# Retention of a chunk in 64-token halves on 64x64 quarters of TensorE, with a state in mid-chunk

## The chip, the cores and the metric

One core of a Trainium2 chip runs the whole kernel as one program. The metric is the device time of that program in microseconds (us). The kernel before was timed three times; the median is 195.26 us.

## The reference, cut to what matters

Retention (linear attention with a decay per head) over 4 batches, 8 heads, 768 tokens, 64 wide, and then a feed-forward part with a Mish activation:

```
for t in range(S):
    state = gamma[h] * state + outer(k[:, :, t], v[:, :, t])      # one 64x64 state a head
    y[:, :, t] = scale * (q[:, :, t] @ state)
x = y.transpose(0, 2, 1, 3).reshape(3072, 512)
h = x @ w_in                      # 512 x 2048
g = h * tanh(softplus(h))         # mish
out = g @ w_out                   # 2048 x 512
```

## The kernel before, in words

The 768 tokens of a batch are cut into 6 chunks of 128 tokens, so there are 24 chunks; chunks 0, 6, 12 and 18 begin a batch. Block 0 takes four chunks, and ten further blocks take two chunks (256 tokens) each. The retention of the next block is woven into the feed-forward part of the current one. The schedule is manual: each engine executes its instructions in the order in which the program writes them, and tiles of a pool take the buffer that was released first.

Retention of a chunk `g` works with these parts. q and k are cast and scaled by powers of gamma (`cast_q`, `cast_v` on GpSimd; `bring_k` is a GpSimd DMA that casts k) and turned on the DMA (`turn_by_dma`). `scores` (L437) multiplies k by q for each head, 64 rows by 128 columns, with 128 tokens moving; `mask` (L447) multiplies the 128x128 scores of 8 heads by the triangle on VectorE, and this is one instruction of 1024 columns a chunk. `y_two` (L535) then makes y for two chunks in one PSUM tile: `present` (L507) multiplies v by the masked scores (128 rows by 64 columns), `outer_two` makes k^T v of two later chunks (`outer`, L454, also 128x64), and `past` (L488) adds the state of the chunk before times q (64x64). ScalarE copies the whole of y into the tile `xt` (L545). The state goes on by `state_sum` (VectorE, L470) and `state_decay` (GpSimd, L475).

The feed-forward part of a block uses a Strassen-like scheme with seven products in place of eight. `g1_seven` makes h: products named first to seventh, each with a half `.0` and a half `.1` of 8 matmuls with 128 columns moving. `snap` copies a product from PSUM (ScalarE, L699; the one of `fifth.0` on VectorE, L697), `plus` adds it to a later product on VectorE (L709, the steps c11, c22, c12), and `mish_of` applies Mish on ScalarE (L704, the steps g11, g22, g12). The string `ORDER` fixes the order. `seven` then makes the output with seven products of 8 matmuls with 256 columns moving (L830); it needs sums of g that VectorE makes (`sums_a`, L618 and L619; `sums_b`, L792; `sums_c`, L796). `x_sums` (L650) makes sums of x from `xt` for the next block.

Between the steps the dictionaries of `steps_of` and `steps_of_first` call other work at named places: `at1` to `at6` within `g1_seven`, and `g7`, `m1`, `m5`, `m6`, `m2`, `m7`, `m3` within `seven`. In the kernel before, `m1` holds the scores of the next block, `m7` holds `y_two` and `m3` holds `x_sums`. PSUM has a pool `mmps` of 4 tiles of one bank (tag mm) and a pool `atps` of 2 tiles of two banks (tag at).

Of the kernel before, what the change touches and what calls it, by code (L numbers as in the profile page):

```python
# [16 lines left out]
def kernel(  # L17
# [9 lines left out]
    nc = tc.nc  # L27
# [29 lines left out]

    cpool = ctx.enter_context(tc.tile_pool(name="rn_const", bufs=1))
# [37 lines left out]

    tri_first = cpool.tile([P, R, C], FP32, name="tri_first")
# [9 lines left out]
    for h in range(H):  # L107
        o = 64 * (h % 2)
        nc.vector.memset(gcm[o:o + 64, h // 2, o:o + 64], float(gamma[h] ** C))
        nc.vector.memset(gcf[o:o + 64, h // 2:h // 2 + 1], float(gamma[h] ** C))  # L110
        o = 64 * (h // HP)
        nc.vector.memset(gcv[o:o + 64, h % HP:h % HP + 1], float(gamma[h] ** C))
    decay = gcv.unsqueeze(2).broadcast_to((P, HP, D))
# [7 lines left out]
    stcs = {}  # L121
# [9 lines left out]
    last_ended = []  # L131
# [61 lines left out]
    def cast_wout(s, on_act=0):  # L193
# [5 lines left out]
        for f in range(n, FPS, 2):  # L199
            nc.scalar.copy(t[:, f:f + 2], src[:, f:f + 2])  # L200

# [74 lines left out]

    def toks(c):
        return slice(c * HB, (c + 1) * HB)
# [167 lines left out]

    def mask(g):  # L447
# [6 lines left out]
    def outer(g, u_ps):  # L454
        _, k16, v16, _ = cast[g]
        for j in range(HP):
            for x in range(2):
                nc.tensor.matmul(  # L458
                    u_ps[64 * x:64 * x + 64, j], k16[:, 2 * j + x], v16[:, HP * x + j],
                    start=j == 0, stop=True, skip_group_check=True)  # L460
        us[g] = u_ps

    def state_sum(g):
        u_ps = us.pop(g)
        if g % NCH == 0:
            stcs[g] = stp.tile([P, HP, D], FP16, name="stc", tag="stc")
            nc.vector.tensor_tensor(stcs[g], u_ps, decay, op=ALU.mult)
        else:
            sus[g] = stp.tile([P, HP, D], FP32, name="suc", tag="suc")
            nc.vector.tensor_tensor(sus[g], u_ps, stcs[g - 1], op=ALU.add)  # L470
# [54 lines left out]
    def handed_on(blk):  # L525
        return [g for g in (first[blk] + 1, first[blk] + 2) if g < NCK and not last_of_batch(g)]

    def outer_two(blk):
        gs = handed_on(blk)
        if gs:  # L530
            u_ps = u_tile()
        for j, g in enumerate(gs):
            outer(g, u_ps[:, j, :, :D])

    def y_two(blk):  # L535
# [4 lines left out]
        outer_two(blk)  # L540
        for j in range(2):
            if (a + j) % NCH > 0:
                past(a + j, lambda i: y_ps[:, i, j])
        xts[blk] = xtp.tile([P, HP, TB], FP16, name="xt")
        nc.scalar.copy(  # L545
            xts[blk][:, :, :2 * C], y_ps.rearrange("p i j c -> p i (j c)"))
# [18 lines left out]
    def xt(blk, bp):  # L565
        return xts[0][:, :, bp] if blk == 0 else xts[blk][:, bp, :BLOCKS[blk] * C]
# [79 lines left out]
    def x_part(blk, i, j):  # L646
        n = NBP // 2
        return xts[blk][:, i * n:(i + 1) * n, j * P:(j + 1) * P]

    def x_sums(blk):  # L650
# [7 lines left out]

    ORDER = """
        first.0 second.0 at1 c11.0 first.1 second.1 g11.0 at2 c11.1 sixth.0 g11.1 fifth.0 at3  # L660
        sixth.1 fifth.1 seventh.0 c22.0 third.0 c12.0 g22.0 g12.0 at4
        seventh.1 c22.1 third.1 c12.1 g22.1 g12.1 at5 fourth.0 at6"""
    def g1_seven(blk, steps):
        n = NBP // 2
        gt = gtiles[blk, 0] = gp.tile([P, NFB, 2 * P], FP16, name="g", tag="g")
        for fb in range(NFB):
            gts[blk, fb] = gt[:, fb]
        both = atps.tile([P, 2, FPS, P], FP32, name="h_ps", tag="at")
        pb, px, pe, px1 = [
            mmps.tile([P, FPS, P], FP32, name="h_ps", tag="mm") for _ in range(4)]  # L670
        pb, px, pe = [pb, both[:, 0]], [px, px1], [pe, both[:, 1]]
# [66 lines left out]
        def _(g):  # L738
            mm(pe, g, s(1), t(1), True)
            m5[g] = snap(pe[g], g == 0)  # L740
# [57 lines left out]
    def seven(blk, steps, last, rest):  # L798
# [3 lines left out]
        px = [mmps.tile([P, wide], FP32, name="o_ps", tag="mm") for _ in range(parts)]  # L802
        if last:
            pe = atps.tile([P, 2, d_model], FP32, name="o_ps", tag="at")
            pb, pe = pe[:, 0, :hf], pe[:, 1, :hf]
        else:
            pe = mmps.tile([P, hf], FP32, name="o_ps", tag="mm")
# [28 lines left out]
        def snap(o_ps):  # L836
            x = op.tile([P, hf], FP32, name="snap", tag="snap", bufs=3)
# [4 lines left out]
        def store_now(i, j, c):  # L842
            row0, c = (first[blk] + i) * P, slice(j * hf + c.start, j * hf + c.stop)
            nc.sync.dma_start(out[row0:row0 + P, c], osb[i][:, c])

        def done(i, j, o_ps, plus=None):
            dst = osb[i][:, j * hf:(j + 1) * hf]
            for t, c in pieces(o_ps):
                if plus is None:
                    nc.vector.tensor_copy(dst[:, c], t)  # L850
# [12 lines left out]
        step("m1")  # L863
        rest()
        if not last:
            pb = mmps.tile([P, hf], FP32, name="o_ps", tag="mm")
# [5 lines left out]
        step("m6")  # L872
        mm(pb, a(0, 1), b(1, 0), True)
        done(0, 0, pb, m1)
# [7 lines left out]
        if last:  # L882
            def end(t, c):
                nc.vector.tensor_copy(osb[1][:, c], t)
                store_now(1, 0, c)

            mm(px, a(1, 1), tm(4), then=end)
        else:
            mm(px, a(1, 1), tm(4))
            done(1, 0, px)  # L890
            for i in range(2):
                row0 = (first[blk] + i) * P
                stores.append((1 + i, out[row0:row0 + P], osb[i]))


# [151 lines left out]
    def first_g2():  # L1047
# [5 lines left out]
        m5 = [op.tile([P, hf], FP32, name="snap", tag="snap", bufs=3) for _ in pairs]  # L1053
# [97 lines left out]
        for p, i in ends:  # L1151
            if (p, i) == (0, 1):
                y_two(1)
            end(p, i, 1)
            if (p, i) != ends[-1]:
# [4 lines left out]
        last_ended.append(lambda: ended(*ends[-1]))  # L1160
# [5 lines left out]

    def sum_next(g):
# [95 lines left out]
```

## Time and profile before

| | |
|---|---|
| median of 3 runs | 195.26 us (194.86 to 377.15) |
| time of the profiled execution | 195.58 us |
| its span | 193.6 us |
| PE busy | 186.7 us (96%) |
| VectorE busy | 162.0 us (84%) |
| ScalarE busy | 119.5 us (62%) |
| GpSimd busy | 91.5 us (47%) |
| granted clock | 1.0 |

The span runs from the first to the last instruction in the trace; the time of the execution has some 2 us more around it. PE is TensorE's matmuls, PEld its weight loads, DVE is VectorE, ACT ScalarE, POOL GpSimd, SP the engine that issues most DMAs.

### The profile page before, as it was taken

The numbers are of one execution on the slowest core, as the hardware profiler recorded it, in microseconds if no ns is written. First come the engines' busy times: TensorE is split into PE (matmuls) and PEld (weight loads), VectorE is DVE, ScalarE is ACT, GpSimd is POOL, SyncE is SP. The second block draws the span as 40 slices with busy tenths as digits, with TensorE's granted clock in tenths as the row PEclk, the third lists the DMA queues.
The fourth block names the chain that finished last, engine by engine and source line by source line (L and its number), as shares of the span: only waits on it lengthen the run. The fifth ranks groups of instructions, "written<-read, shape, count | busy, mean of one in ns | idle before, by whom it ended". The sixth has DMA issues, their size and how long they took to land.

```text
span 193.6 us, 6554 instructions
## 1 busy us (share of the span) xinstructions
PE 186.7 (96%) x2722; PEld 157.6 (81%) x2722; DVE 162.0 (84%) x329; ACT 119.5 (62%) x217; POOL 91.5 (47%) x135
## 2 busy tenths in 40 slices
PE   6999999999999999999999999999999999999992
PEld 2467645885988988988988988988988988988982
DVE  3787799989798997897897997897897997897871
ACT  3464798463793692782782882882873863964950
POOL 4280206596657756916905907907807914110000
PEclk9999999999999999999999999999999999999999
DMA  5999999995899999995995996994995993201103
GB/s 166 351 372 405 404 408 249 308 247 57 118 204 240 132 314 227 177 183 142 187 183 135 203 158 150 185 193 129 175 188 145 191 138 77 94 0 61 51 3 108
DMA packets 95805, 36.10 MB, mean 187 GB/s; under 512 B 82592, under 2 KB 89376, under 8 KB 95776
## 3 DMA queue, kind: packets, MB, share of 16 engines
q1 hardware_dynamic: 74544, 33.04, 67.2%
q0 software_dynamic: 21088, 2.62, 22.3%
q8 instruction: 21, 0.34, 0.7%
q14 instruction: 8, 0.07, 0.1%
q10 hardware_dynamic: 144, 0.03, 0.1%
HBM read 27.30 MB, written 6.29 MB: 174 GB/s over the span
## 4 chain that ended last, share of the span: by engine, by line
PE 85%; DVE 8%; issue 2%; ACT 1%; POOL 0%; POOLq 0%; DVEq 0%
PE h_ps L689 32%; PE o_ps L830 32%; PE o_ps L1072 5%; PE y_ps L512 3%; PE at L443 3%; DVE wsum L643 3%; PE at L419 2%; PE o_ps L1131 2%; PE h_ps L922 2%; PE y_ps L503 1%; DVE am L295 1%; PE u_ps L458 1%; DVE win L190 1%; DVE hsum L709 1%; DVE wout L198 1%
## 5 line engine op out<-in xcount | busy, mean ns | idle before, releaser
L709 DVE TENSOR_TENSOR hsum<-h_ps,hsnap 128x512 f32<-128x512 f32 x60 | 38.5, 685 | 6.0 <-PE h_ps L689 3.7
L704 ACT ACTIVATE g<-hsum 128x512 f16<-128x512 f32 x60 | 36.9, 631 | 4.0 <-DVE hsum L709 4.0
L699 ACT COPY hsnap<-h_ps 128x512 f32<-128x512 f32 x50 | 28.1, 583 | 14.8 <-PE h_ps L689 14.8
L689 PEld LDWEIGHTS <-wsum 128*128 128x128 f16 x640 | 36.4, 98 | 0.4
L830 PEld LDWEIGHTS <-gsum 128*128 128x128 f16 x336 | 30.3, 98 | 4.4 <-DVE gsum L618 0.5
L689 PE MATMUL h_ps<-xsum,wsum 128*128 128x128 f16 x480 | 30.4, 219 | 0.0
L830 PE MATMUL o_ps<-tmat,gsum 128*128 128x256 f16 (+1 forms) x256 | 29.7, 266 | 0.2 <-DVE gsum L618 0.2
L689 PEld LDWEIGHTS <-win 128*128 128x128 f16 x480 | 28.1, 98 | 1.4
L388 POOL DMA_DIRECT2D qk<-in_k_dram x36 | 27.9, 776 | 0.0
L401 POOL COPY gate<-gsum 128x1 f16<-128x1 f16 x18 | 3.4, 186 | 50.8 <-DVE gsum L792 39.7
L545 ACT CAST xt<-y_ps 128x1024 f16<-128x1024 f32 x10 | 10.1, 1012 | 25.2 <-PE y_ps L503 22.2
L830 PEld LDWEIGHTS <-g 128*128 128x128 f16 x256 | 23.4, 98 | 2.3
L449 DVE TENSOR_TENSOR am<-at,tri 128x1024 f16<-128x1024 f32 x20 | 24.3, 1218 | 0.3 <-PE at L443 0.3
L393 POOL TENSOR_TENSOR v<-vf,qvs 128x512 f16<-128x512 f32 x20 | 21.3, 1067 | 2.0 <-DMA vf<-in_v_dram 1.9
L852 DVE TENSOR_TENSOR osb<-o_ps,snap 128x256 f32<-128x256 f32 (+1 forms) x31 | 12.0, 412 | 11.5 <-ACT xt L545 9.8
L376 POOL TENSOR_TENSOR qk<-qf,qvs 128x512 f16<-128x512 f32 x20 | 21.4, 1068 | 0.0
L830 PE MATMUL o_ps<-wout,g 128*128 128x256 f16 (+1 forms) x168 | 20.8, 267 | 0.0
L689 PE MATMUL h_ps<-xt,win 128*128 128x128 f16 x320 | 19.5, 219 | 0.0
L839 ACT COPY snap<-o_ps 128x256 f32<-128x256 f32 (+1 forms) x32 | 11.4, 358 | 6.3 <-PE o_ps L830 6.3
L689 PE MATMUL h_ps<-xsum,win 128*128 128x128 f16 x160 | 12.3, 220 | 0.0
L689 PE MATMUL h_ps<-xt,wsum 128*128 128x128 f16 x160 | 12.2, 219 | 0.0
L704 ACT ACTIVATE g<-h_ps 128x512 f16<-128x512 f32 x20 | 11.9, 595 | 0.0
(124 smaller groups left out, 282.8 us busy)
## 6 DMA issues: line engine op xcount, KB each, us to landing
vf<-in_v_dram SPq DMA_DIRECT2D x24, 256.0 KB, 5.0
out_dram<-osb SPq DMA_DIRECT2D x22, 256.0 KB, 4.4
qf<-in_q_dram SPq DMA_DIRECT2D x20, 256.0 KB, 4.4
wi<-in_moe_w_in_dram SPq DMA_DIRECT2D x3, 1024.0 KB, 10.6
wt<-in_moe_w_out_dram SPq DMA_DIRECT2D x3, 1024.0 KB, 8.8
qk<-in_k_dram POOLq DMA_DIRECT2D x36, 64.0 KB, 4.1
qfirst<-in_q_dram SPq DMA_DIRECT2D x2, 512.0 KB, 4.4
kf<-in_k_dram SPq DMA_DIRECT2D x4, 256.0 KB, 5.0
```

The lines of the kernel that those rows point to most:

```text
L376: nc.gpsimd.tensor_tensor(by_head(g, room16(g)[0]), by_head(0, loaded[g][0]), f.broadcast_to((P, 2, HP, D)), op=ALU.mult)
L388: nc.gpsimd.dma_start(room16(g)[1][:, x::2], src[:, HP * x:HP * x + HP])
L393: nc.gpsimd.tensor_tensor(room16(g)[2], loaded[g][2], vs.unsqueeze(2).broadcast_to((P, H, D)), op=ALU.mult)
L449: nc.vector.tensor_tensor(am, ats.pop(g), tri.unsqueeze(1).unsqueeze(1).broadcast_to((P, 2, HP, C)), op=ALU.mult)
L545: nc.scalar.copy(xts[blk][:, :, :2 * C], y_ps.rearrange("p i j c -> p i (j c)"))
L689: nc.tensor.matmul(h_ps[g][:, f], w(g, f, d), x(d), start=first and f == 0 and d == 0, stop=d == n - 1, skip_group_check=True)
L699: nc.scalar.copy(x, h_ps)
L704: nc.scalar.activation(gt[:, fb:fb + FPS, j * P:(j + 1) * P], h, AF.Mish, scale=inv_boost3)
L709: nc.vector.tensor_tensor(h, h_ps, x, op=ALU.add)
L830: nc.tensor.matmul(t, x(f), w(f)[:, c], start=first and f == 0, stop=f == n - 1, skip_group_check=True)
L839: nc.scalar.copy(x[:, c], t)
L852: nc.vector.tensor_tensor(dst[:, c], t, plus[:, c], op=ALU.add)
```

## The change

The two chunks of a block are worked in 64-token halves `c` = 0, 1.

- Scores: `scores_two` makes only the two diagonal 64x64 squares of each chunk's 128x128 scores, for both chunks into one PSUM tile, and `mask_two` masks both chunks in one VectorE instruction of 1024 columns.
- State in mid-chunk: `outers` makes k^T v for each half of a chunk. `state_midway` adds the first half's to the state before the chunk (a new VectorE instruction, 256 columns), and `state_sum` adds the second half's to that. The first chunk of a batch adds to a tile of zeros (`none`).
- y: `y_of` multiplies q of each half by the state before that half, adds v times the masked square, and makes the outer products of the next two chunks (two `mm` tiles) at the same place. All these matmuls are 64x64 with 64 tokens moving. Rows 0 to 63 and 64 to 127 write different PSUM banks, so y of half of the tiles is made in two parts: ScalarE copies one part (`rest`, 512 columns), VectorE adds it to the other (`y_end`, 512 columns); ScalarE copies the remaining half of y (512 columns).
- Tokens: the 256 tokens of a block are now in the order (half, chunk, 64 tokens); `rows` gives the rows of the output for the stores.
- Feed-forward: the second half's `pb` and `pe` tiles move from `mmps` to a second `atps` tile, since two `mm` tiles now hold outer products from `m7` to `at3` of the next block. `fifth.0`'s snap moves to ScalarE, g11.1 comes later in `ORDER`, the last copy of a block (`done(1, 0)`) moves to ScalarE. In the last block one product is made earlier, and the last product to be made is another one.
- GpSimd: two casts of v and one `bring_k` move to `at3`, ahead of the block's second half.
- Block 2 (`TURN`) and block 1 have steps of their own, which make the outer products of chunks 7 and 9 beside the scores. `ended` of the first block's last two products moves from its end to `at3` of block 1.

The core of the diff:

```diff
+    def outers(gs, pool, tag):
+        u_ps = [pool.tile([P, 2, HP, D], FP32, name="u_ps", tag=tag) for _ in range(2)] if (
+            pool is mmps) else atps.tile([P, 2, 2, HP, D], FP32, name="u_ps", tag=tag)
...
+            for j in range(HP):
+                for c in range(2):
+                    for x in range(2):
+                        if c == 0 or not last_of_batch(g):
+                            nc.tensor.matmul(
+                                us[g][c][64 * x:64 * x + 64, j], k16[toks(c), 2 * j + x],
+                                v16[toks(c), HP * x + j], start=True, stop=True,
+                                skip_group_check=True)
+    def scores_two(blk):
...
+                for c in range(2):
+                    for x in range(2):
+                        o = slice(64 * x, 64 * x + 64)
+                        nc.tensor.matmul(
+                            at[toks(c), x, n, j], kt[o, j, toks(c)], qt[o, j, toks(c)],
+                            start=True, stop=True, skip_group_check=True)
+    def y_of(blk):
...
+        for n in range(2):
+            qt = qkts[a + n][0]
+            state = state_before(a + n), mids[a + n]
+            for j in range(HP):
+                e = slice(64 * (j % 2), 64 * (j % 2) + 64)
+                for c in range(2):
+                    for x in range(2):
+                        o = slice(64 * x, 64 * x + 64)
+                        nc.tensor.matmul(
+                            whole[e, x, int(x != c), j // 2, n], state[c][o, j],
+                            qt[o, j, toks(c)], start=fresh(0, x, j % 2), stop=x != c,
+                            skip_group_check=True)
...
+                            y[e, x, 0, j // 2, n], cast[a + n][2][toks(c), HP * x + j],
+                            am[toks(c), x, n, j], start=not same and fresh(1, x, j % 2),
+                            stop=True, skip_group_check=True)
+        present_of(False, other)
+        rest = hp.tile([P, 2, HP // 2, 2, HB], FP32, name="hsum", tag="hsum", bufs=3)
+        nc.scalar.copy(rest, other[:, :, 0])
+        present_of(True, whole)
+        gs = outers_at(blk)
+        if gs:
+            outers(gs, mmps, "mm")
...
+        nc.scalar.copy(to[:, :2], whole[:, :, 0])
+        yet.append(lambda: nc.vector.tensor_tensor(to[:, 2:], whole[:, :, 1], rest, op=ALU.add))
...
+    def state_midway(g):
+        mids[g] = stp.tile([P, HP, D], FP16, name="stm", tag="stm", bufs=2)
+        nc.vector.tensor_tensor(mids[g], us[g][0], state_before(g), op=ALU.add)
...
     ORDER = """
-        first.0 second.0 at1 c11.0 first.1 second.1 g11.0 at2 c11.1 sixth.0 g11.1 fifth.0 at3
-        sixth.1 fifth.1 seventh.0 c22.0 third.0 c12.0 g22.0 g12.0 at4
-        seventh.1 c22.1 third.1 c12.1 g22.1 g12.1 at5 fourth.0 at6"""
+        first.0 second.0 at1 first.1 c11.0 g11.0 second.1 at2 c11.1 sixth.0 fifth.0 sixth.1 at3
+        fifth.1 g11.1 seventh.0 c22.0 third.0 c12.0 seventh.1 c22.1 g22.0 third.1 c12.1 g12.0
+        g22.1 g12.1 at5 fourth.0 at6"""
...
-            m5[g] = snap(pe[g], g == 0)
+            m5[g] = snap(pe[g])
...
+        if last:
+            pz = mmps.tile([P, hf], FP32, name="o_ps", tag="mm")
+            mm(pz, a(1, 1), tm(4), True)
+            z = snap(pz)
         rest()
...
+        if last:
+            mm(pe, s(4), b(1, 1))
+            done(0, 1, pe, u2)
+            mm(px, s(3), tm(3))
+            done(1, 1, px, m5)
+            done(1, 0, px, z)
...
+            mm(pb, a(0, 1), b(1, 0), True, then=end)
+            return
...
-            "at1": [*then((gate_x, blk), (cast_q, a)), (sum_next, a - 3), (decay_next, a - 3),
-                   (cast_v, a), (bring_k, a + 1)],
+            "at1": [*then((gate_x, blk), (cast_q, a))],
             "at2": [(store_due, 1), (turn_and_load, a)],
-            "at3": [(store_due, 2), (sum_next, a - 2)],
+            "at3": [*only((state_midway, a - 1), (state_sum, a - 1), (decay_next, a - 1)),
+                    (cast_v, a), (store_due, 2), (cast_v, a + 1), (bring_k, a + 1)],
...
-            "m1": only((scores, a - 2), (scores, a - 1), (mask, a - 2)),
-            "m5": [(sums_b, blk), *only((gate_g, blk), (decay_next, a - 2))],
-            "m6": [*only((mask, a - 1)), (sums_c, blk), *then((gate_s, blk)),
-                   (cast_q, a + 1), (cast_v, a + 1), (bring_k, a + 2)],
+            "m1": only((scores_two, nb)),
+            "m5": [*only((mask_two, nb)), (sums_b, blk)],
+            "m6": [(sums_c, blk), *then((gate_s, blk)), (cast_q, a + 1), (bring_k, a + 2)],
             "m2": [(turn_and_load, a + 1)],
-            "m7": only((y_two, nb)),
-            "m3": only((x_sums, nb)),
+            "m7": [*only((y_of, nb)), *then((state_midway, a), (state_sum, a), (decay_next, a))],
+            "m3": only((y_end,)),
+            "m4": only((x_sums, nb)),
```

More of the change, by code (lines that the diff above doesn't have):

```diff
@@ L447, in mask, with y_end @@
+    def y_end():
+        yet.pop()()
     def mask(g):
@@ L801, in seven @@
         wide = hf // parts
[L802 to L807, printed above, removed]
+        px, pe = [mmps.tile([P, hf], FP32, name="o_ps", tag="mm") for _ in range(2)]
         osb = [op.tile([P, d_model], FP32, name="osb", tag="osb") for _ in range(2)]
@@ L842, in store_now @@
         def store_now(i, j, c):
[L843 to L844 removed]
+            c = slice(j * hf + c.start, j * hf + c.stop)
+            nc.sync.dma_start(rows(blk, i)[..., c], osb[i][:, c])
         def done(i, j, o_ps, plus=None):
@@ L881, in seven @@
         step("m3")
[L882 to L893, printed above, removed]
+        mm(px, a(1, 1), tm(4))
+        done(1, 0, px)
+        step("m4")
+        for i in range(2):
+            stores.append((1 + i, rows(blk, i), osb[i]))
     def load_weights():
```

174 lines of the change are left out of this document (118 added, 56 removed).

## The prediction

> **What bounds the kernel now.** I read the page first, then the chain that ended last in order of time, then the timelines of a middle block by engine, and last the table of stretches.
>
> ```profile
> PE 186.7 (96%) x2722; PEld 157.6 (81%) x2722; DVE 162.0 (84%) x329; ACT 119.5 (62%) x217; POOL 91.5 (47%) x135
> PE 85%; DVE 8%; issue 2%; ACT 1%; POOL 0%; POOLq 0%; DVEq 0%
> 63.35:177.24 113.89, 113.89 (x1811) 103.79 (x1809) 99.58 (x200) 73.23 (x136) 59.93 (x91) 1.00 0.91 157
> ```
>
> PE is the bound. In the stretch from 63.35 to 177.24 us, which is blocks 2 to 9, PE is busy all of 113.89 us at the full granted clock (1.00), so nothing is to be won there except PE time itself, and any new wait of PE costs its full length. One block in the chain (start, length, what):
>
> ```profile
> 106.24 5.81 PE h_ps L689 x104
> 112.04 0.87 PE o_ps L830 x8
> 112.92 0.55 PE at L443 x16
> 113.47 0.55 PE h_ps L689 x8
> 114.02 3.49 PE o_ps L830 x32
> 117.52 0.57 PE y_ps L512 x16
> 118.08 0.25 PE u_ps L458 x16
> 118.33 0.35 PE y_ps L503 x16
> 118.68 1.85 PE o_ps L830 x16
> 120.53 5.81 PE h_ps L689 x104
> 132.38 0.12 PE u_ps L458 x8
> 104.15 0.24 PE y_ps L503 x8
> ```
>
> The block takes 14.29 us (106.24 to 120.53). Its retention is scores 0.55, present 0.57, outer 0.25 and past 0.35. The last two rows are the same work in other blocks, half as many.
>
> **PE: the price of a matmul and of a tile change.** Eight more matmuls of past cost 0.35 - 0.24 = 0.11 us, which is 0.057 for each four (64x64, 128 columns moving), so its first eight should cost 0.115 and the remaining 0.12 is the change of tile size. The other changes agree: 8 matmuls L689 take 5.81/104 x 8 = 0.447 within the long run and 0.55 behind the scores (0.10 more); 16 of L830 take 2 x 0.87 = 1.74, and 1.85 behind past (0.11). I take 0.11 us a change. Outer, with 64 columns moving, costs 0.25/16: two 128x64 matmuls in 0.031 us. How four quarters run shows where the timeline is cut short:
>
> ```profile
> 75.61 0.25 PE L503 MATMUL y_ps<-qkt,stc 64*64 64x128 f16 x4
> 20.95 0.44 PE L328 MATMUL u_ps<-v,qk 64*64 64x64 f16 x16
> ```
>
> The first row is a window 0.018 us wide, with four matmuls begun in it: four quarters start together, and a quarter is held for the time of its own columns. The second is 64x64 with 64 moving on two quarters only. What isn't shown is four quarters with 64 moving. Bounds: 0.031 us for four (outer's and L328's pace for a pair, which loads and streams through the array as much as four quarters do) and 0.057 (past's four with 128 moving). I take 0.031, since outer already fills the whole array at that pace.
>
> **PE: the sum.** Before, a full block has 0.55 + 0.57 + 0.25 + 0.35 + the two returns 0.10 + 0.11 = 1.93 us. Over the nine blocks 2 to 10 whose retention changes that is 17.4; past is halved in the three that begin a batch (-0.35), outer is halved in two and missing in one (-0.5): 16.5. After, a block has 32 scores, 32 past, 32 present and mostly 32 outer matmuls, thus 8 groups of four each. Zeros are multiplied where a batch begins, so past is never halved; outer is 17 chunks of 4 groups. In all 9 x 24 + 68 = 284 groups at 0.031 = 8.9, and 4 changes in nine blocks at 0.11 = 4.0: 12.9 us. **PE saves 3.6 us**: 2.6 of it streaming, 1.0 a change of tile size less a block.
>
> **ScalarE and the sums of g: a new wait.** The work of a block on the other engines, by these groups:
>
> ```profile
> L449 DVE TENSOR_TENSOR am<-at,tri 128x1024 f16<-128x1024 f32 x20 | 24.3, 1218 | 0.3 <-PE at L443 0.3
> L697 DVE COPY hsnap<-h_ps 128x512 f32<-128x512 f32 x10 | 6.9, 690 | 0.2
> L470 DVE TENSOR_TENSOR suc<-u_ps,stc 128x256 f32<-128x256 f32 x12 | 5.0, 416 | 0.0
> L850 DVE COPY osb<-o_ps 128x256 f32<-128x256 f32 x9 | 3.8, 418 | 0.0
> L709 DVE TENSOR_TENSOR hsum<-h_ps,hsnap 128x512 f32<-128x512 f32 x60 | 38.5, 685 | 6.0 <-PE h_ps L689 3.7 <-ACT hsnap L699 1.1
> L699 ACT COPY hsnap<-h_ps 128x512 f32<-128x512 f32 x50 | 28.1, 583 | 14.8 <-PE h_ps L689 14.8
> L545 ACT CAST xt<-y_ps 128x1024 f16<-128x1024 f32 x10 | 10.1, 1012 | 25.2 <-PE y_ps L503 22.2 <-PE y_ps L494 3.0
> ```
>
> VectorE loses a mask (1.22), the snap of fifth.0 (0.69) and a copy (0.42), and gains `y_end` (0.69, as L709) and, for L470's two, four additions (2 x 0.42): some 0.8 us less a block. ScalarE gains the snap (0.58) and the copy (about 0.37), and two copies of 0.58 replace one of 1.01: 1.1 us more. Its mean load allows that (62%), but its queue between the first sum and the last Mish does not:
>
> ```profile
> 107.48 1.45 DVE L709 TENSOR_TENSOR hsum<-h_ps,hsnap 128x512 f32<-128x512 f32 x2
> 108.19 0.63 ACT L704 ACTIVATE g<-hsum 128x512 f16<-128x512 f32 x1
> 109.72 1.06 ACT L699 COPY hsnap<-h_ps 128x512 f32<-128x512 f32 x2
> 111.07 2.42 ACT L704 ACTIVATE g<-hsum 128x512 f16<-128x512 f32 x4 [0.29 <-DVE hsum L709]
> 113.54 0.42 DVE L618 TENSOR_TENSOR gsum<-g 128x512 f16<-128x512 f16 x1
> 105.81 0.35 DVE L654 TENSOR_TENSOR xsum<-xt 128x256 f16<-128x256 f16 x1
> 106.61 0.28 DVE L657 TENSOR_TENSOR xsum<-xt,xsum 128x256 f16<-128x256 f16 x1
> ```
>
> Queued copies follow each other by 1.06 - 0.58 = 0.48 us and Mish by (2.42 - 0.63)/3 = 0.60. Times from the block's first matmul (106.24): before, the first Mish starts at 1.95, the last four run from 4.83 to 7.25, and the second half of `sums_a`'s s1 ends at 113.96, which is 7.72. PE needs it after 4 matmuls of `mm(pe, s(1))`, 114.02 + 0.44 = 8.22: half a microsecond to spare. After: `y_end` waits for `done(0, 1)`, whose product ends 0.87 before the block's end and shows 0.2 later; with 0.34, 0.69 and x_sums (105.81 to 106.89, 1.08) c11.0 starts at about 1.4 and the first Mish at 2.13. Behind it in the queue lie four copies (0.54 + 3 x 0.48), then g11.1 and the four: 4.58, 5.18, ..., 6.98, the last ends at 7.6, and s1 at 8.05. PE comes there at 5.81 + 0.87 + scores 0.36 + 0.55 + 0.44 = 8.03. So the half microsecond is gone and **PE waits some 0.07 us**. Next is late s2 behind it, and s3 (L792), which now stands behind the single mask: from s1's end 0.34 + 0.03 + 1.13 + 0.68 = 2.2 us, against PE's 0.44 + 2 x 0.87 = 2.2. I take 0.1 us a block, 0 to 0.3, in eight blocks: **+0.8**. `mid`, `state_sum` and `y_end` ahead of x_sums are hidden by PE's last two products (1.74 us); without them c11.0 would be late by the same amount.
>
> **GpSimd, the DMA of k, and the end.**
>
> ```profile
> 108.64 0.62 POOL L475 TENSOR_TENSOR stc<-suc,gcv 128x256 f16<-128x256 f32 x1
> 109.22 1.04 POOL L393 TENSOR_TENSOR v<-vf,qvs 128x512 f16<-128x512 f32 x1
> 110.20 1.55 POOL L388 DMA_DIRECT2D qk<-in_k_dram  x2
> DMA to landing us min/median/max: 3.0/4.1/6.2
> 187.95 3.08 SPq L844 DMA_DIRECT2D out_dram<-osb  x5
> L844 SPq DMA_DIRECT2D out_dram<-osb x5: 332/333/401, 187.9 to 190.6; - x5
> 190.10 0.29 DVE L884 COPY osb<-o_ps 128x128 f32<-128x128 f32 x1 [0.15 <-PE o_ps L830]
> 185.02 1.50 PE L830 MATMUL o_ps<-tmat,gsum 128*128 128x256 f16 x20 [0.19 <-DVE gsum L618]
> 48.66 6.25 PE h_ps L689 x104
> ```
>
> The k of chunk a+1 was issued at 3.96 us in the block and first used by the transpose at the block's end; now the outer products of the same block need it, at about 11.9. In its queue it stands at `at3` behind the new `state_decay` wait (VectorE's two additions end near 3.65), the decay and two casts of v (0.57 + 2 x 0.98): its DMAs start at 6.2 and 7.0, and land 4.1 later (median) at 11.1, at 13.2 with the longest. The median is 0.8 early; behind the waiting outer products stand the block's last two products and all of the next block. I put 0.2 us for all blocks together, among them block 2 whose loads are late; 0 to 5.
>
> At the end, the early product takes PE's one wait (0.19) and three split products are whole again: -0.25. But (1,1) and (1,0) now come together just before the two last pieces, so SP issues four stores in a row, at 0.33 to 0.40 and some 0.1 between them. Before, the last store starts at 187.95 + 3.08 - 0.40 = 190.63, 0.5 behind the start of the copy it waits for; I expect 1.0. **+0.25** (0 to 0.6). Block 1's first part holds 0.44 us more than a later block's (6.25 against 5.81), where the first block's last sums meet its own; the change moves them to `at3`, into ScalarE's full queue, so I count nothing, -0.4 to +0.4. The new constants on GpSimd stand behind the triangle that PE waits for at the start, so they cost nothing.
>
> **Sum.** -3.6 + 0.8 + 0.2 + 0.25 = -2.35 us from the profiled execution's 195.58 (span 193.6 and 2.0 around it): 193.2. That execution is 0.3 above the median of the runs, so the forecast is **192.9 us**, 1.2% faster. Its own range, from the terms, is 191.5 to 194.6.
>
> **Rivals.**
>
> *A. The waits don't come.* If ScalarE's queue packs 0.1 us better, or y is ready earlier, the 0.8 goes and the time is 192.1; with block 1's 0.4, k's 0.2 and the end's 0.25 as well it is 191.2. For it: the new wait is a difference of two long sums; against it: s1, s2 and s3 all come out on the edge. 0.2.
>
> *B. Not four quarters at once.* In `y_of` the states come in the order c, x with the same column half, so each quarter is hit twice in a row, and past may run on two quarters at a time. Then its 72 groups cost double: +2.25, 195.2. Against it: the next head takes the other column half, so pairs may overlap. If the same held for all the quarters, at 0.057, the streaming gain would be lost: 284 x 0.026 = +7.4, less the 0.8 of waits that a later PE no longer has: 199.5. 0.11 for the first, 0.03 for the second.
>
> *C. k lands late.* At a landing of 5.5 us, PE waits 0.6 in each of eight blocks: +4.8, 197.7. For it: the DMA engines are busy (share 0.91 in the stretch above). Against it: the median. 0.09.
>
> *D. Slower: each instruction has a price.* The change doubles the matmuls of a block, from 64 to 128, in all 1112 in the nine blocks. If one costs 0.0144 us whatever it does (past, 0.115 for 8), they take 16.0 + 4.0 = 20.0 against 16.5; at outer's 0.0156, 21.3. That is 3.5 to 4.8 slower in place of 3.6 faster, and with the end 199 to 200.3. It decides above (16.5 - 4.0)/1112 = 0.0112 us. Against it: the row with four starts in 0.018 us. 0.07.
>
> The Trainium skill speaks for D: its page TensorE: Matmul & The Clock Gate (section Back-to-back issue gap) gives a matmul of 1 to 64 columns an issue floor of about 25 ns, whatever its width. By that the 1112 would take 28 us and the kernel some 15 us more than before (an estimate from that page); the trace's pace of 0.014 to 0.016 us for matmuls on several tiles does not agree with it.
>
> **How the numbers follow.** The forecast has 0.50; A 0.20, B 0.14, C 0.09, D 0.07. Two per cent of the time, 3.9 us, is about what a measurement of this kernel can tell from no change: below 191.4 or above 199.2. Faster by that is the half of A in which the other terms vanish too: 0.10. Slower is most of D and the second of B: 0.08. The remaining 0.82 is within it. The range 191.0 to 196.4 leaves out D, most of C and the second of B, some 0.17.
>
> **What would show it.** In the profile after, the scores should take about 0.36 us a block and the whole of y with the outer products about 0.9; 1.1 is B for past alone, and 1.5 or more is B for all or D. A block should take 13.9 to 14.0 in place of 14.2 to 14.3, with PE idle some 0.1 before L830 for gsum; none is A. A wait of PE for k by DMA at the outer products is C. The last store should start 1.0 after the last addition starts. I am wrong if blocks are below 13.8 or above 14.2.

## The result, and the profile after

The kernel after takes 235.17 us (233.80 to 239.61) where the kernel before takes 195.45 in the same series: a ratio of 1.2021 with a 95% interval of 1.1923 to 1.2119. It is 20% slower; 192.9 was forecast, in a range up to 196.4. The profiled execution took 233.8 us. For the fourth experiment below no ratio is given, because three of its four runs, the profiled one among them, were some 2% longer than the fastest, and only the place of a wait is read from its profile.

The page of the kernel after: busy times, the rows of the clock and of the DMA engines over the span, and the shares of the chain that ended last.

```profile
PE 195.1 (84%) x3298; PEld 160.9 (69%) x3298; DVE 160.1 (69%) x327; ACT 127.1 (55%) x245; POOL 93.7 (40%) x134
PEclk9999999999999999999799999889979958999955
DMA  6999999899999999998998969999999761101111
PE 35%; DMA 35%; DVE 9%; POOL 6%; SPq 5%; issue 3%; ACT 1%; POOLq 0%; DVEq 0%
```

Before, 85% of the chain was PE. Now PE has 35% and DMA as much, and the granted clock falls below full speed in places. The stretches (length, busy time of PE, weight loads, VectorE, ScalarE, GpSimd, clock, DMA share, GB/s) say where the 38.3 us of span went. A DMA share can stand above 1, because the times of packets overlap (up to 20 are under way at once at the end of the kernel before). First the kernel before, blocks 2 to 8 and then 9 to the end; then the kernel after, the same two; last a piece of its end.

```profile
63.35:163.19 99.84, 99.84 (x1595) 91.04 (x1593) 87.14 (x175) 64.11 (x119) 58.57 (x88) 1.00 1.01 171
163.19:194.15 30.96, 26.68 (x417) 24.68 (x413) 22.58 (x48) 17.34 (x35) 1.36 (x3) 1.00 0.18 60
```

```profile
65.37:191.47 126.10, 106.25 (x2026) 92.35 (x2026) 85.50 (x171) 67.88 (x137) 57.74 (x81) 0.94 1.19 135
191.47:232.57 41.10, 26.91 (x440) 24.93 (x438) 19.50 (x42) 19.03 (x39) 0.00 (x0) 0.83 0.12 40
219.00:231.00 12.00, 0.00 (x0) 0.00 (x0) 0.00 (x0) 0.00 (x0) 0.00 (x0) 0.56 0.13 42
```

Blocks 2 to 8 take 26.3 us more (126.10 against 99.84): PE is idle for 19.9 of them and busy for 6.4 more, at a clock of 0.94 in place of 1.00. The end takes 10.1 more (41.10 against 30.96), and 1.9 lie ahead of block 2. In its last piece no engine computes for 12 us, and the stores alone keep the DMA busy at a share of 0.13: two engines of sixteen are 0.125. The two move 42 GB/s, so one store of 256 KB needs 6.2 us of them, and the two stores of a block 12.5 us of a block that took 14.2 before.

What PE waits for (in all, times, longest), and the chain through a block and a half (start, length, what):

```profile
PE u_ps L473 <- DMA qk<-in_k_dram: 15.0, 11, 4.8
```

```profile
130.79 0.62 POOL stc L581
131.41 0.90 SPq L421
...
132.36 0.57 SPq L155
...
132.98 7.17 DMA vf<-in_v_dram
...
140.28 1.04 POOL v L409
141.32 0.74 POOL qk L404
142.06 7.26 DMA qk<-in_k_dram
...
149.36 0.47 PE u_ps L473 x8
149.84 0.42 DVE stm L571
```

The outer products wait for k by DMA, as in rival C, but for up to 4.8 us and not 0.6. The chain is a loop: the load of v (7.17 us) is issued behind the transpose on SP, the cast of v waits for it, the DMA of k (7.26) is issued behind the cast, PE waits for k, and the next transpose waits, here, for GpSimd's decay of the state behind PE; in earlier passes of the chain it waits for k's landing itself. Between issue and landing, the DMAs of k took (those of the tile of q and k begun from 60 us on, to 175 us before and to 190 us after), before and then after:

```profile
DMA to landing us min/median/max: 2.7/4.0/6.5
```

```profile
DMA to landing us min/median/max: 3.5/7.2/10.9
```

So the transfers of k became longer, and the load of v in the chain is as long. Which comes first, the loop or the slow transfers, the experiments had to tell.

### The profile page after: what moved, and what is told of

It is laid out like the page before. It is cut to its first block, busy times and chain, and to the rows that moved or that the text cites. A ratio compares the mean times of both kernels' runs of the same rounds, so it can differ in the third digit from the quotient of the medians.

```text
span 231.9 us, 7753 instructions
## 1 busy us (share of the span) xinstructions
PE 195.1 (84%) x3298; PEld 160.9 (69%) x3298; DVE 160.1 (69%) x327; ACT 127.1 (55%) x245; POOL 93.7 (40%) x134
## 4 chain that ended last, share of the span: by engine, by line
PE 35%; DMA 35%; DVE 9%; POOL 6%; SPq 5%; issue 3%; ACT 1%; POOLq 0%; DVEq 0%
DMA qk<-in_k_dram 19%; DMA vf<-in_v_dram 16%; PE h_ps L793 11%; PE o_ps L929 11%; PE o_ps L1178 4%; SPq L421 3%; POOL v L409 3%; DVE wsum L745 2%; POOL qk L404 2%; PE at L435 2%; SPq L155 2%; PE o_ps L1237 2%; PE h_ps L1028 2%; DVE am L311 1%; PE u_ps L473 1%
## 5 line engine op out<-in xcount | busy, mean ns | idle before, releaser
L803 ACT COPY hsnap<-h_ps 128x512 f32<-128x512 f32 x60 | 32.2, 592 | 5.5 <-PE h_ps L793 4.9
L929 PE MATMUL o_ps<-tmat,gsum 128*128 128x256 f16 x240 | 30.3, 273 | 1.4 <-DVE gsum L720 1.4
L949 ACT COPY osb<-o_ps 128x256 f32<-128x256 f32 x9 | 3.4, 372 | 36.0 <-PE o_ps L929 36.0
L581 POOL TENSOR_TENSOR stc<-suc,gcv 128x256 f16<-128x256 f32 x15 | 9.7, 646 | 29.9 <-DVE suc L576 23.3
L473 PE MATMUL u_ps<-v,qk 64*64 64x64 f16 x264 | 7.0, 202 | 17.4 <-DMA qk<-in_k_dram 15.0
L929 PE MATMUL o_ps<-wout,g 128*128 128x256 f16 (+1 forms) x168 | 20.8, 267 | 0.0
L951 DVE TENSOR_TENSOR osb<-o_ps,snap 128x256 f32<-128x256 f32 x30 | 12.6, 421 | 8.1 <-PE o_ps L929 4.5
L473 PEld LDWEIGHTS <-qk 64*64 64x64 f16 x264 | 4.8, 110 | 19.1 <-DMA qk<-in_k_dram 16.2
L571 DVE TENSOR_TENSOR stm<-u_ps,stc 128x256 f16<-128x256 f32 x15 | 6.3, 418 | 15.7 <-PE u_ps L473 15.7
L938 ACT COPY snap<-o_ps 128x256 f32<-128x256 f32 x31 | 11.4, 370 | 7.9 <-PE o_ps L929 7.4
L538 ACT COPY hsum<-y_ps 128x512 f32<-128x512 f32 x9 | 5.3, 585 | 18.4 <-PE y_ps L531 18.4
```

What stands on the lines that cost most here:

```text
L473: nc.tensor.matmul(us[g][c][64 * x:64 * x + 64, j], k16[toks(c), 2 * j + x], v16[toks(c), HP * x + j], start=True, stop=True, skip_group_c ...
L581: by.tensor_tensor(stcs[g], sus.pop(g), decay, op=ALU.mult)
L803: nc.scalar.copy(x, h_ps)
L929: nc.tensor.matmul(t, x(f), w(f)[:, c], start=first and f == 0, stop=f == n - 1, skip_group_check=True)
L938: nc.scalar.copy(x[:, c], t)
L951: nc.vector.tensor_tensor(dst[:, c], t, plus[:, c], op=ALU.add)
```

## The experiments

Two theories stand in the expectations below. L: the order of the queues makes the loop, and the loop makes k late. S: the stores are the cause, since `rows` writes each store of a full block to two places of 64 rows (two chunks, one half of each) where the kernel before wrote 128 consecutive rows. The first four runs were made under L. Their Theory D says that the DMA engines are busy and k is late whatever stands ahead of it; it has nothing to do with rival D of the prediction. Theory K and rival P are told where they first stand.

**k ahead of the casts of v.** The loop is cut between v and k:

```diff
-                    (cast_v, a), (store_due, 2), (cast_v, a + 1), (bring_k, a + 1)],
+                    (bring_k, a + 1), (cast_v, a), (store_due, 2), (cast_v, a + 1)],
```

> One edit of the changed kernel: on GpSimd, bring_k(a+1) stands ahead of the two casts of v, no longer behind them (at3; at1 in block 2). Theory L (a loop in the queues: k lands, then SP turns that chunk and only then issues the load of a later v, then GpSimd casts that v and only then issues the next k; its length of about 19 us takes the place of PE's 14 as the block's period): k no longer waits for v, the loop is cut, 193 to 197 us, and no long wait of PE at the outer products. Theory D (the DMA engines are busy, and a k that is needed at 12 us in the block lands late whatever stands ahead of it): k is issued 2 us sooner at most, so PE still waits some us a block, 215 to 230 us.

234.07 us, ratio 1.1922 (1.1848 to 1.1995). Nothing is won: the time is far from L's range, and above D's too.

**Loads ahead of the transpose.** The loop is cut between the transpose and the loads on SP (`load_to(g + 3)` ahead of `turn_by_dma(g)`).

> Another cut through the same loop in the changed kernel: on SP the loads of a later chunk are issued ahead of the transpose of this chunk, no longer behind it. GpSimd's order stays, so k is still issued behind both casts of v. Theory L: v is there long before its cast, the casts run on time and k is issued at about 6 us in the block and lands at 10 to 13: 193 to 200 us, some short waits at the outer products. Theory D: the DMA work and k's place are the same, 225 to 236 us.

237.54 us, ratio 1.2121 (1.2047 to 1.2194). Nothing is won here either, and the time is again above D's range.

**The kernel before with GpSimd's new order.** `cast_v` for both chunks and `bring_k` of the second move to `at3`, and nothing else changes.

> The kernel before with one part of the change alone: GpSimd's order (both casts of v and then bring_k(a+1) at at3) in the steps of blocks 2 to 10; PE's, VectorE's and ScalarE's work is as before, with outer products that need no k of that chunk. Theory L: the loop lies in the queues of SP, GpSimd and DMA and needs nothing of the new matmuls; PE meets it at the scores, which wait for the transpose: 215 to 235 us if the loop alone is longer than a block. If the loop is short at the latencies of before (k 4.1, v 4.8 us: some 13 us) and only grows once DMAs are bunched, 194 to 200 us. Theory D in its narrow form (only outer products that need k in the same block can be late): 195 us, no change.

197.34 us, ratio 1.0094 (1.0062 to 1.0126). The new order costs 1.7 us, not 40: L's second range, for a short loop. In its profile PE waits for sums of g (0.2 us before), not for k:

```profile
PE o_ps L830 <- DVE gsum L618: 0.8, 3, 0.4
PE o_ps L830 <- DVE gsum L792: 0.5, 2, 0.2
```

**Both cuts at once, k still earlier.** `bring_k` goes to `at1`, the loads go ahead of the transpose.

> Both cuts at once in the changed kernel: bring_k(a+1) back at at1, behind the cast of q, and SP's loads ahead of the transpose. It leaves the rest of the change, thus the prediction's own sum without waits for k. By that sum 192.7 us (191.5 to 194.6), with PE idle some 0.1 us a block before the products that need the sums of g, and the last store 0.5 us later behind its addition than before. Theory D: 210 to 230 us.

232.0 to 237.3 us. The waits of PE in its profile:

```profile
PE at L487 <- DMA qkt<-qk: 20.8, 6, 5.7
PE u_ps L473 <- DMA qk<-in_k_dram: 0.2, 1, 0.2
```

The wait for k is gone (0.2 us), and the time is as it was, above both forecasts: PE now waits for the transposes. Theory L falls. Whatever is late last is only where a general lateness shows, and so the stores came under suspicion. The next four runs were put together to try them.

**The kernel after with plain stores.** The rows of the output are left in the new order of tokens, everything else is as in the kernel after:

```diff
-        if blk <= FIRST:
-            return r[i * P:(i + 1) * P]
-        return r.rearrange("(n c t) d -> c n t d", n=2, c=2)[i]
+        return r[i * P:(i + 1) * P]
```

> The changed kernel with its stores written as before: each store of 128 rows goes to 128 rows that follow each other in the output (this leaves the rows in the changed order of tokens), no longer to two pieces of 64 rows. Nothing else is changed, GpSimd's and SP's orders neither. Theory S (a store whose outermost dimension has only two pieces is run by two of the 16 DMA engines; two such stores a block hold these two engines for 2 x 64 x 0.084 = 10.8 us in place of 1.4, and every transpose and load, which has its share on all 16, waits behind them): 191 to 196 us, and k lands within 4 to 5 us. Theory L (the loop over k, transpose, load of v and cast): the orders are the same, so 230 to 236 us.

196.72 us, ratio 1.0061 (1.0029 to 1.0093). 38.5 of the 39.7 us are gone with one edit of a store's address, and k lands after 4.3 us (median). The time is 0.7 above S's range; the runs with k early come back to that.

**The kernel before with stores in two pieces.** The other way round: the kernel before, with `rows` of the kernel after for its stores and no other edit.

> The kernel before with the changed kernel's stores alone: blocks 2 to 10 store each 128 rows to two pieces of 64 rows 128 apart (the rows of the output are in another order than the tokens). Theory S: the same two engines are overloaded, so 220 to 240 us, with late transposes and k. Theory L, or any cause in the retention's own work: 195 to 197 us.

229.62 us, ratio 1.1709 (1.1623 to 1.1796). The stores alone make the kernel before 34 us slower. Its wait of PE, and the issues of k with their median time to landing, which was 4.1 before:

```profile
PE at L449 <- DMA qkt<-qk: 14.9, 5, 5.2
```

```profile
qk<-in_k_dram POOLq DMA_DIRECT2D x36, 64.0 KB, 7.0
```

That kernel doesn't need k early; there PE waits for the transposes. Theory S is shown from both sides.

**Two ways around it**, with the rows where the reference has them. The first issues a store as two of 64 rows each (`put`, one DMA for each chunk). The second keeps one DMA, but interleaves the tokens of the two chunks in `xt`, so that the store's slowest count is 64:

```diff
-        return r.rearrange("(n c t) d -> c n t d", n=2, c=2)[i]
+        return r.rearrange("(n c t) d -> c t n d", n=2, c=2)[i]
...
-        to = xts[blk][0].rearrange("p b i (n t) -> p b i n t", n=2)
+        to = xts[blk][0].rearrange("p b i (t n) -> p b i n t", n=2)
```

> The changed kernel with each store of two pieces issued as two stores of 64 rows. The rows go where the changed kernel puts them. Theory S: 64 rows spread over all 16 engines, so 191.5 to 196 us; SP issues 24 more DMAs, which may cost a little at the end (two more issues of some 0.4 us behind the last addition). Theory L: 230 to 236 us.

200.93 us, ratio 1.0310 (1.0266 to 1.0354). Most of the loss is gone, but this is 4.9 above S's range. Much of what is left shows at the end: in its profile SP issues the last ten stores over 6.44 us and is done 4.9 us behind the last addition, where the kernel with plain stores issues five over 2.67 us and is done after 1.1. Some 0.8 for two more issues had been expected.

> The changed kernel with another order of tokens within a half: the two chunks' tokens alternate, so that a store's outermost dimension has 64 pieces (of two rows each) and it stays one DMA; ScalarE's and VectorE's copies of y write with a step of two elements. Theory S: 191.5 to 195 us, the prediction's own sum (192.7) with up to 0.3 us a block if the stepped writes are slower. Theory L: 230 to 236 us.

197.97 us, ratio 1.0128 (1.0101 to 1.0155). A store of this kernel goes from one place to the other with every row, and the time is 1.25 us above the plain rows: pieces as such are not what is dear. That is still 3.0 above S's range, and more than the expected 0.3 us a block for the stepped writes. It still waits 2.0 us for k at one place, so the next four runs put k early in the two healthy kernels.

**k early, with healthy stores.** `bring_k(a + 1)` goes to `at1`, and in block 2 ahead of the casts of v: first with the interleaved tokens, then with the plain rows of the fifth run (rows in the new order of tokens).

> The kernel with interleaved tokens (stores of 64 pieces), and bring_k(a+1) ahead of the casts of v: at1 behind the cast of q in blocks 3 to 10, first of the three in block 2. Theory K (what is left of the loss, after the stores, is k landing late for the outer products in blocks 2 and 3, because it stands behind casts that wait for v; some 3 us in all): 195 to 196 us, with no wait of PE for k. Rival: the waits only move to v, whose cast the same outer products need: 197.5 to 198 us.

196.45 us, ratio 1.0045 (1.0020 to 1.0070). PE no longer waits for k; the time is 0.45 above K's range.

> The same place of bring_k in the kernel whose stores are in one piece (rows left in the changed order of tokens), so neither two-piece stores nor stepped writes: the prediction's own sum, without what it left out. If the sum is right 192.5 to 193.8 us; theory K says it comes from waits in blocks 2 and 3 going away, so 3 us below the 196.7 of the same kernel with k behind the casts. Rival: v is late instead, 196 to 197 us.

195.17 us, ratio 0.9991 (0.9968 to 1.0013), against 196.72 without the early k: 1.55 us. PE's waits for k (1.8 us at three places in the fifth run) are gone. Theory K had 3 us, the sum 192.5 to 193.8 and the rival 196 to 197, and the time lies between them. As long as the stores were slow, the same place of k (in the fourth run, with the loads ahead of the transpose) won nothing.

**ScalarE's queue.** From the interleaved kernel, `fifth.0`'s snap goes back to VectorE (`m5[g] = snap(pe[g], g == 0)`).

> The kernel with interleaved tokens and early k, and the snap of fifth.0 back on VectorE, as before the change. The prediction's term for ScalarE's queue (0.1 us of PE waiting for the sums of g in each of eight blocks, since that copy moved to ScalarE): the waits go, 0.5 to 0.8 us below the kernel with early k. Rival: PE does not wait there, or VectorE's queue is as full: within 0.3 us of it.

197.07 us, ratio 1.0077 (1.0052 to 1.0101): 0.6 slower than with the snap on ScalarE, which is hardly more than the scatter (the two intervals overlap). Neither the term nor its rival had a slower kernel. VectorE has 75.31 us of work in 84.00 us of its blocks, against ScalarE's 58.12, and PE is busy for 83.39:

```profile
92.50:176.50 84.00, 83.39 (x1710) 74.72 (x1709) 75.31 (x150) 58.12 (x113) 40.95 (x57) 1.00 0.93 145
```

With the snap on ScalarE, PE is busy for all of the same 84.00 us, and VectorE for 70.75.

**Loads ahead of the transpose again**, now with healthy stores:

> The kernel with interleaved tokens and early k, and SP's loads of a later chunk ahead of the transpose. If the casts of v are what is late in blocks 2 and 3 (they waited 2.4, 1.1 and 3.7 us for v there), they come sooner and it is 0.5 to 1.5 us below the kernel with early k alone. If only k mattered, no change, or up to 1 us slower because transposes come later.

196.38 us, ratio 1.0033 (1.0007 to 1.0059): no difference from 196.45, as expected if only k mattered.

**How many engines, or how many pieces.** The kernel before, with its stores cut into 4, 8 and 16 pieces (`n=4`, `n=8`, `n=16` in `rows`), rows in another order of tokens:

> The kernel before, its stores in 4 pieces of 32 rows each instead of 128 consecutive rows (rows of the output in another order). Theory S (the outermost count of a store's pattern is the number of DMA engines that carry it): in the run before with two pieces the last stretch with nothing but stores moved 43 GB/s, so a store of 256 KB took 6.1 us of two engines and a block's two stores 12.2 us of them; on four engines it is 6.1 us a block, about half. I expect well below the 229.6 of two pieces and above the kernel before: 198 to 212. Rival P (each extra piece of a store costs, whatever number of engines): four pieces are at least as slow as two, 229 or more.

> The same with 8 pieces of 16 rows (rows in another order). Theory S: eight engines, 3.0 us a block on each against 1.5 with sixteen: 195.5 to 199. Rival P: 229 or more.

> The same with 16 pieces of 8 rows (rows in another order). Theory S: sixteen engines as before, 195 to 196, though a store has 16 pieces. Rival P: 229 or more.

| pieces of a store | us | ratio |
|---|---|---|
| 1 (128 rows) | 195.38 | 1 |
| 2 | 229.62 | 1.1709 (1.1623 to 1.1796) |
| 4 | 203.01 | 1.0335 (1.0245 to 1.0424) |
| 8 | 197.01 | 1.0075 (1.0052 to 1.0097) |
| 16 | 196.18 | 1.0026 (0.9994 to 1.0058) |

More pieces cost less, and sixteen cost no time that can be told from the scatter. With four pieces the end of the kernel, where nearly nothing but stores is left, shows a share of 0.21 and 66 GB/s, with nothing moved in its first us; four engines of sixteen are 0.25:

```profile
192.00:200.00 8.00, 1.96 (x28) 1.70 (x25) 1.33 (x5) 0.00 (x0) 0.00 (x0) 0.95 0.21 66
```

The packets say it more directly. Each trace ends with the same five stores of the last block (two of 64 KB, three of 128 KB); here are the packets of the last 12, 8 and 7 us with two pieces (the kernel after), with four, and in the kernel before:

```profile
DMA packets 628, 0.50 MB, mean 42 GB/s; under 512 B 10, under 2 KB 628, under 8 KB 628
DMA packets 660, 0.52 MB, mean 66 GB/s; under 512 B 20, under 2 KB 660, under 8 KB 660
DMA packets 720, 0.52 MB, mean 75 GB/s; under 512 B 80, under 2 KB 720, under 8 KB 720
```

The packets under 512 B are thus 2, 4 and 16 for each store; with eight pieces they are 8 (40 in all), and with sixteen 16 (80). By the start and length of each packet in the trace, exactly two are under way for 78% of the 12 us at the end of the kernel after, and with four pieces four for half of the 8 us above.

So the slowest count of the pattern, up to sixteen, sets how many engines carry a store. The Trainium skill says this as a rule: in DMA: Bandwidth & Descriptors, section "Why a DMA increments its semaphore by 16 and not by 1", the number of engines is the largest number up to 16 that divides the slowest dimension of both patterns. The shares of 0.13 and 0.21, the table and the packets agree with it. All counts tried here are powers of two, so no run tests that it is a divisor.

**y interleaved by TensorE.** The interleaved kernel pays 1.3 us against the plain rows. Here TensorE writes y with a stride of two in PSUM, so that the copies need none:

```diff
+        def of(y, n):
+            return y.rearrange("p n t -> p (n t)").rearrange("p (t n) -> p n t", n=2)[:, n]
...
-                            whole[e, x, int(x != c), j // 2, n], state[c][o, j],
+                            of(whole[e, x, int(x != c), j // 2], n), state[c][o, j],
```

> The interleaved tokens of f1, but TensorE writes y with a stride of two in PSUM, so that ScalarE and VectorE copy y without one. f1 took 196.45 and the same kernel with plain rows and no interleaving (f2) 195.17. If the strided copies of y (ScalarE and VectorE writes of 2 bytes every 4) are what costs the 1.3 us, it goes to 195.0 to 195.5. If the stores' order of rows costs it (each store now jumps between two places in DRAM), it stays at 196.2 to 196.8. If TensorE is slower writing with a stride, it is above 197.

198.38 us, ratio 1.0135 (1.0078 to 1.0191). The copies did get faster, and PE slower. First rows of the interleaved kernel with k early, then of this one (busy time, mean ns of one), and the chain of this one:

```profile
L545 ACT CAST xt<-y_ps 128x512 f16<-128x512 f32 x9 | 6.7, 743 | 0.0
L546 DVE TENSOR_TENSOR xt<-y_ps,hsum 128x512 f16<-128x512 f32 x9 | 6.5, 726 | 0.0
```

```profile
L548 ACT CAST xt<-y_ps 128x512 f16<-128x512 f32 x9 | 5.3, 592 | 0.0
L549 DVE TENSOR_TENSOR xt<-y_ps,hsum 128x512 f16<-128x512 f32 x9 | 6.1, 680 | 0.0
```

```profile
104.33 0.58 PE y_ps L523 x32
104.90 0.45 PE y_ps L534 x32
105.35 0.25 PE u_ps L473 x32
```

The strided copy costs ScalarE 0.15 us (743 against 592 ns), and the strided write costs PE 0.58 + 0.45 - 0.38 - 0.33 = 0.32 us a block in y, by the rows of y in the next section. The outer products behind it take 0.25 in place of 0.34, so that 0.23 us a block are left. What costs the interleaved kernel its 1.3 us stays open: in the two profiles with k early only 0.29 us of it lies in blocks 4 to 9 (84.18 against 83.89), and PE does not wait there.

No version is clearly faster than the kernel before.

## Why the prediction was wrong

**The step that failed is one that isn't there.** The prediction costs each tile change, matmul, copy and wait of the change, and k's DMA; the stores' new rows stand in the description of the change and have no term in the sum. They were put at nothing, and no reason is given. What the runs showed in their place is 34 us in the kernel before (229.62 against 195.38) and 38.5 in the kernel after (235.17 against 196.72). The profile of before had what was needed to ask: 22 stores of 256 KB, 16 of which the change writes in two pieces, as it does the five smaller ones of the last block, and DMA engines at a share of 0.91 in blocks 2 to 9. With k's DMA the rivals did look for a late landing, and C named the wait that came. Its price was far too low (0.6 us in each of eight blocks, thus 4.8, against 26.3 us in seven, 15.0 of them PE's waits for k), since C took a landing of 5.5 us, close to the pace of before, where the median after was 7.2. Cutting what C rests on did not help (first and fourth run), so C was right on where the wait shows and not on why. The chance of slower, 0.08, had been put on PE's price for each instruction.

With the stores healthy and k early, the steps can be read one by one, in the kernel with plain rows (195.17 us, span 192.9). Its stretches: block 1, 2, 3, blocks 4 to 9, and the last with the end; then the same of the kernel before.

```profile
47.96:62.79 14.83, 14.53 (x299) 13.01 (x297) 13.37 (x28) 10.40 (x21) 10.84 (x16) 1.00 1.22 188
62.79:77.16 14.37, 14.34 (x308) 13.14 (x306) 12.18 (x26) 9.85 (x21) 10.27 (x15) 1.00 1.18 220
77.16:92.21 15.05, 14.31 (x298) 12.74 (x296) 12.70 (x25) 9.80 (x20) 9.35 (x13) 1.00 1.25 172
92.21:176.10 83.89, 83.89 (x1731) 76.38 (x1729) 70.68 (x147) 59.48 (x120) 40.98 (x58) 1.00 0.99 145
176.10:193.57 17.47, 12.43 (x177) 11.59 (x173) 9.44 (x22) 9.12 (x19) 0.00 (x0) 0.98 0.18 62
```

```profile
48.66:63.35 14.69, 14.69 (x228) 13.02 (x225) 12.90 (x26) 9.48 (x19) 9.60 (x14) 1.00 1.17 187
63.35:77.88 14.53, 14.53 (x235) 13.18 (x233) 12.70 (x27) 9.25 (x17) 9.35 (x15) 1.00 1.26 219
77.88:92.05 14.17, 14.17 (x227) 12.92 (x225) 12.43 (x26) 9.12 (x17) 8.38 (x14) 1.00 0.94 170
92.05:177.24 85.19, 85.19 (x1355) 77.69 (x1353) 74.45 (x149) 54.87 (x102) 42.21 (x64) 1.00 0.85 144
177.24:194.15 16.91, 12.63 (x200) 11.92 (x197) 10.14 (x23) 8.22 (x18) 0.00 (x0) 1.00 0.18 63
```

**PE's price: right in kind, too low in y.** The six undisturbed blocks 4 to 9 gain 85.19 - 83.89 = 1.30 us, 0.22 each, which is 2.0 for nine in place of 3.6. A block takes 13.98, inside the 13.9 to 14.0 that was forecast, but by luck: the wait of 0.1 that did not come hides a part of what PE is slower. The chain of the same kernel:

```profile
69.92 0.26 PE at L485 x32
113.02 0.38 PE at L485 x32
117.44 0.38 PE y_ps L518 x32
117.82 0.33 PE y_ps L529 x32
104.11 0.34 PE u_ps L471 x32
```

In block 2 the scores follow outer products of the same tile size: 0.26/8 = 0.033 us for four, where 0.031 was taken, and 0.38 - 0.26 = 0.12 is the tile change, where 0.11 was taken. But y with the outer products takes 1.05 in place of 0.9: without one change that is 0.93/24 = 0.039 for four. That is the mis-sized term. It comes near the 1.1 of rival B for past alone, but not from past, which takes 0.38 - 0.12 = 0.26 like the scores: it is present (0.33) and outer (0.34), at (0.33 + 0.34)/16 = 0.042 for four. That is not outer's own pace: in the last run above, behind a slower present, the same 32 take 0.25, which is the forecast 0.031 for four. Why stays open. At 0.26/32 = 0.008 us a matmul D is refuted. The issue floor of about 25 ns, which the Trainium skill gives in TensorE: Matmul & The Clock Gate (section Back-to-back issue gap), does not hold for matmuls on four quarters here, at 8 ns each.

**ScalarE's queue: the wait didn't come.** In blocks 4 to 9 PE is busy for all of 83.89 us, so the 0.1 us a block for sums of g does not show, as in rival A. ScalarE was also the wrong engine to fear: with the snap back on VectorE the kernel was not faster, and rather slower.

**k and GpSimd's order: too cheap.** With healthy stores the early k wins 1.55 us, the price of issuing it behind the casts of v; 0.2 was forecast, with bounds of 0 to 5.

**The loads of blocks 1 and 2.** Block 3 takes 0.88 us more than before, and the first block ends 0.70 earlier (0.82 from the first instruction). In the kernel with plain rows GpSimd waits 3.73 us for v in block 2, and its next work comes late; the trace then shows a VectorE sum of x at 0.70 us, whose likes take 0.28, while GpSimd's decay runs beside it, and PE short of a sum of g for 0.61 us. No run tried this, so that it explains the 0.88 stays an argument. Why the first block is shorter, where nothing was counted, no run tried either.

```profile
72.98 1.04 POOL L407 TENSOR_TENSOR v<-vf,qvs 128x512 f16<-128x512 f32 x1 [3.73 <-DMA vf<-in_v_dram]
77.74 0.74 POOL L579 TENSOR_TENSOR stc<-suc,gcv 128x256 f16<-128x256 f32 x1
77.93 0.70 DVE L756 TENSOR_TENSOR xsum<-xt 128x256 f16<-128x256 f16 x1
86.06 0.61 PE L927 MATMUL o_ps<-tmat,gsum 128*128 128x256 f16 x4 [0.61 <-DVE gsum L718]
```

**The end.** The last block and the end take 17.47 in place of 16.91, +0.56 where +0.25 (0 to 0.6) was forecast.

With the first block's -0.82 (counted from the first instructions, at 0.67 and 0.55) the parts add up: -0.82 + 0.14 - 0.16 + 0.88 - 1.30 + 0.56 = -0.70, and the spans differ by 0.7 (192.9 and 193.6). The sum had 2.35. Of the 1.65 between them PE's price is 1.6 more and block 3 1.1 (it lost 0.88 instead of winning 0.22), while ScalarE's wait (0.8) did not come and the first block (0.8) is shorter; the rest is small.

## What to carry to other kernels

A change that reorders tokens also reorders the rows of every store and load: write down the pattern of each DMA before and after, slowest count first, and cost it, even where the bytes are the same. Here a slowest count of 2 in place of 128 put all of a block's stores on two of sixteen engines, and everything else that passes these two came late: k, v and the transposes alike (that they share these two engines is worked out from the pattern and from the late landings; the trace does not name a packet's engine). Where cutting one wait only moves it to the next (k's 15.0 us to the transposes' 20.8), look for what makes all transfers slow, and try the suspect alone in the kernel before: that one run said 34 of the 40 us.

## What the hardware showed that was not expected

- The time of stores goes with the slowest count of their pattern: 229.6, 203.0, 197.0 and 196.2 us for 2, 4, 8 and 16 pieces of the same 256 KB.
- TensorE is slower when it writes PSUM with a stride of two: 64x64 matmuls on four quarters take 0.58 us for 32 in place of 0.38, and 0.45 in place of 0.33.
- Two stores of 64 rows, one after the other, are 4.2 us slower than one of 128 rows (200.93 against 196.72), although neither has a slowest count under 64. In the profiles SP takes 6.44 us to issue the last ten, against 2.67 for the last five; why an issue takes longer stays open.
